# A layernorm, long-convolution and feed-forward kernel: Strassen's seven products in the first feed-forward product, 512-column second product, chunks of two tiles

## The chip, the cores and the metric

The kernel runs on one core of a Trainium2 chip. The metric is the device time of one execution in microseconds (us); the kernel before was timed in three runs, which gave a median of 1087.03 us (1082.56 to 1088.22). All values are float32. TensorE (PE) multiplies, VectorE (DVE), ScalarE (ACT) and GpSimd (POOL) work on elements, and SyncE (SP) issues most transfers. Matmuls write to PSUM, whose eight banks of 512 float32 columns are the scarce resource in what follows.

## The reference

```python
x  = A_q                                    # [1, 2048, 576]
xn = _layernorm(x)                          # over the last axis
# A: q * (long causal convolution of (short convolution of k) * v, plus kv * ssm_D)
k_shift = sum(k_pad[:, t:t + S, :] * shift_k[:, ks - 1 - t] for t in range(4))
kv = k_shift * v
y  = irfft(rfft(kv, 2S) * rfft(ssm_k, 2S))[:, :S] + kv * ssm_D
# B: feed-forward, 576 -> 4608 -> 576
h  = jnp.maximum(jnp.einsum("bsd,df->bsf", xn, w1), 0)
out = x + xn * y + jnp.einsum("bsf,fd->bsd", h, w2)
```

## The kernel before

**Products in three passes.** A float32 factor is held as two fp32r parts, a high one (`hi`, `h1`, `hh`) and the rest (`lo`, `l1`, `ll`). A product of two such factors is three matmuls: high by high, high by low, low by high. ACT makes the high part by a copy, and DVE or POOL subtracts it from the source to make the low part. ACT and DVE read results out of PSUM.

**Feed-forward.** The 2048 rows of x are 16 tiles of 128 rows, in four blocks of four tiles (`b`); two blocks make a half. The 4608 hidden columns go in 12 chunks (`ci`) of three tiles of 128 (`FT = 3`), and each half of the rows passes over all of them, so that there are 24 chunk passes. For each chunk, block and tile `mm1` (L322) makes a transposed hidden tile [128 hidden, 512 rows]: the 576 input columns are four contraction tiles of 128 and a remainder of 64, which takes 4 x 3 + 2 = 14 matmuls of 512 columns (L334, output `psh`). ACT applies the ReLU into `hh` (L339) and DVE makes `ll` (L340). `mm2` (L344) multiplies a row tile's hidden part by the chunk's three tiles of w2: two column halves of 288, each 3 x 3 = 9 matmuls (L358, output `pso`), and DVE adds each half into `acc` in SBUF (L362 for a half's first block, L366 otherwise). The `mm2` of a block run while the next block's `mm1` do.

**Operands.** `make_xT` (L244) takes statistics of four row tiles (L168), normalizes (L183), transposes on PE (L269) into `psf` and splits the columns (L203, L204); `first_xT` (L212) does this for the first block, with a centring that does not wait for the standard deviation, whose reciprocal is applied later at L362. `split_w1` and `split_w2` (L306, L315, and POOL at L277) make the weights' two parts, one chunk ahead; `load_w1` and `load_w2` refill the single raw buffer on SP's queue.

**The convolution.** `conv` (L411) is a generator that does the long convolution as an FFT by matmuls in four stages: `fk` transforms the kernel, `fx` makes the short convolution and the gate (DVE at L483 to L492) and transforms it, `fm` multiplies in the middle (32 groups, L562, with ACT copies at L583 to L617), `fo` transforms back (L700, L701), multiplies by the normalized x and adds. Stages hand over through DRAM (`zx`, `zk`, `zy`). For the row tiles of the second half, which `fo` does first, the result is added into `acc` (L673), where the feed-forward also adds.

**What sets the order.** `tick` advances `conv` by a share of the matmul columns issued, so that its pieces lie between the feed-forward's in program order. The tile scheduler then orders each engine by a simulated timeline, within the data dependencies; on the chip each engine runs its own list in order. PSUM has two banks for `psh`, three for `pso` and three for `psf`.

## Time and profile before

| | us |
|---|---|
| median of 3 runs | 1087.03 (1082.56 to 1088.22) |
| span of the profiled execution | 1084.4 |
| TensorE busy | 1070.8 (99% of the span) |
| VectorE busy | 732.5 (68%) |
| ScalarE busy | 585.0 (54%) |
| GpSimd busy | 261.9 (24%) |

A row of a group view reads: line, engine, operation, output <- inputs, sizes, count, then busy time in us and the mean in ns of one. Matmuls overlap each other in PE's pipeline, so that a matmul's own duration is longer than the spacing of two; spacings are read from stretches of the chain or the timeline. DVE's operations overlap by a little too: the groups add up to some 770 us where 732.5 are busy. The window view gives, for each stretch, its length, the busy time of PE, weight loads, DVE, ACT and POOL with instruction counts, the granted TensorE clock as a share of full speed, the share of DMA time and GB/s.

### The profile page before, as it was taken

Reading aid. Unit: us, or ns where it says so; the run is one execution under the profiler, and the core shown is the slowest. Engines: PE = TensorE matmul, PEld = TensorE weight load, DVE = VectorE, ACT = ScalarE, POOL = GpSimd, SP = SyncE. Lnnn points to the kernel's source line nnn. Section 1 sums busy time; section 2 is a strip of 40 time slices with the busy share of each in tenths; the row PEclk is TensorE's granted clock in tenths of the full one; section 3 lists DMA queues with packets and bytes.
Section 4 is the critical chain, followed back from the end, with each engine's and each line's share of the span. In section 5 each row is a group of like instructions: output and inputs, shape, how many; then the busy total and the mean of one; then the engine's idle time right before and its main releaser. Section 6 shows DMA issues by size and latency. Waiting matters only on the chain.

```text
span 1084.4 us, 17301 instructions
## 1 busy us (share of the span) xinstructions
PE 1070.8 (99%) x6537; PEld 977.2 (90%) x6537; DVE 732.5 (68%) x1213; ACT 585.0 (54%) x1184; POOL 261.9 (24%) x218
## 2 busy tenths in 40 slices
PE   8999999999999999999999999999999999999998
PEld 5889899998999999999999999899999999999998
DVE  5423677949998777677666676666656666876774
ACT  4221587823443323333388787888788864543430
POOL 4131222412312322312213031211113032332410
PEclk9999999999999999999999999999999999999999
DMA  9950345664644525325564343434344227745524
GB/s 217 181 145 27 119 147 190 195 185 133 187 138 136 153 77 164 117 60 171 190 182 135 99 135 99 135 99 136 92 143 141 80 103 221 201 130 143 164 81 110
DMA packets 112255, 150.79 MB, mean 139 GB/s; under 512 B 45261, under 2 KB 62927, under 8 KB 112172
## 3 DMA queue, kind: packets, MB, share of 16 engines
q1 hardware_dynamic: 103884, 135.50, 42.0%
q0 software_dynamic: 7968, 13.44, 4.8%
q8 instruction: 52, 0.85, 0.3%
q10 hardware_dynamic: 320, 0.74, 0.3%
q14 instruction: 31, 0.25, 0.1%
HBM read 114.26 MB, written 35.39 MB: 138 GB/s over the span
## 4 chain that ended last, share of the span: by engine, by line
PE 90%; DMA 4%; SPq 2%; DVE 2%; ACT 1%; issue 1%; POOL 0%; ACTq 0%; DVEq 0%
PE pso L358 40%; PE psh L334 39%; PE psf L562 7%; PE psf L398 3%; DMA r<-in_w 3%; SPq L421 2%; PE psf L700 1%; PE psf L701 1%; DMA k-1_2414<-in_k 1%; DMA sk<-in_shift_k 0%; PE psf L269 0%; DVE lok L553 0%; POOL l L277 0%; DVE k L611 0%; DVE lox L553 0%
## 5 line engine op out<-in xcount | busy, mean ns | idle before, releaser
L277 POOL TENSOR_TENSOR l<-r,h 128x640 fp32r<-128x640 f32 (+1 forms) x144 | 224.4, 1563 | 621.8 <-ACT h L306 448.3
L358 PE MATMUL pso<-h,hh 128*128 128x288 f32 x1152 | 337.3, 295 | 3.7 <-ACT hh L339 2.7
L358 PE MATMUL pso<-l,hh 128*128 128x288 f32 x1152 | 338.5, 295 | 0.0
L358 PE MATMUL pso<-h,ll 128*128 128x288 f32 x1152 | 337.7, 295 | 0.0
L334 PE MATMUL psh<-xhi,h 128*128 128x512 f32 x576 | 226.5, 394 | 1.1 <-DVE ll L340 1.1
L334 PE MATMUL psh<-xlo,h 128*128 128x512 f32 x576 | 226.5, 393 | 0.0
L334 PE MATMUL psh<-xhi,l 128*128 128x512 f32 x576 | 225.8, 392 | 0.0
L358 PEld LDWEIGHTS pso<-h,hh 128*128 128x128 f32 x1152 | 215.8, 188 | 10.4 <-ACT hh L339 3.4
L358 PEld LDWEIGHTS pso<-l,hh 128*128 128x128 f32 x1152 | 216.3, 188 | 5.8
L358 PEld LDWEIGHTS pso<-h,ll 128*128 128x128 f32 x1152 | 216.0, 188 | 0.6
L366 DVE TENSOR_TENSOR acc<-pso,acc 128x288 f32<-128x288 f32 x288 | 128.6, 451 | 75.1 <-PE pso L358 72.1
L339 ACT ACTIVATE hh<-psh 128x512 fp32r<-128x512 f32 x144 | 85.6, 595 | 169.1 <-PE psh L334 168.2
L340 DVE SCALAR_TENSOR_TENSOR ll<-psh,hh 128x512 fp32r<-128x512 f32 x144 | 99.0, 687 | 109.8 <-ACT hh L339 109.5
L334 PEld LDWEIGHTS psh<-xhi,l 128*128 128x128 f32 x576 | 108.4, 188 | 20.3
L334 PEld LDWEIGHTS psh<-xhi,h 128*128 128x128 f32 x576 | 108.4, 188 | 17.1 <-DVE ll L340 1.4
L334 PEld LDWEIGHTS psh<-xlo,h 128*128 128x128 f32 x576 | 108.6, 188 | 15.5 <-DVE xlo L204 0.4
L315 ACT ACTIVATE h<-r 128x576 fp32r<-128x576 f32 x72 | 48.9, 682 | 73.4 <-DMA r<-in_w 46.9
L362 DVE SCALAR_TENSOR_TENSOR acc<-pso,rstd,acc 128x288 f32<-128x288 f32 x96 | 48.3, 512 | 27.5 <-PE pso L358 26.5
L392 DVE TENSOR_TENSOR ks<-kt,ks 64x288 fp32r<-64x288 f32 x64 | 57.6, 901 | 3.3 <-ACT ks L391 1.3
L399 ACT ACTIVATE zx<-psf 128x288 f32<-128x288 f32 x64 | 25.8, 407 | 59.3 <-PE psf L398 38.9
L334 PE MATMUL psh<-xhl,l 128*128 128x512 f32 x144 | 56.4, 392 | 0.0
L334 PE MATMUL psh<-xhl,h 128*128 128x512 f32 x144 | 56.2, 391 | 0.0
(109 smaller groups left out, 1451.2 us busy)
## 6 DMA issues: line engine op xcount, KB each, us to landing
r<-in_w SPq DMA_DIRECT2D x24, 864.0 KB, 5.3
r<-in_w SPq DMA_DIRECT2D x23, 768.0 KB, 6.1
zk<-zk SPq DMA_DIRECT2D x32, 288.0 KB, 2.5
zx<-zx SPq DMA_DIRECT2D x32, 288.0 KB, 2.6
ztk<-zk SPq DMA_DIRECT2D x32, 288.0 KB, 3.0
ztx<-zx SPq DMA_DIRECT2D x32, 288.0 KB, 2.8
zy<-vo SPq DMA_DIRECT2D x32, 288.0 KB, 2.1
zo<-zy SPq DMA_DIRECT2D x32, 288.0 KB, 3.0
```

Source lines behind the costliest of these rows:

```text
L277: return nc.gpsimd.tensor_tensor(dst, src, hi, OP.subtract)
L315: nc.scalar.activation(h2, r2[:, j, :], AF.Copy)
L334: nc.tensor.matmul(ps, a, m, start=i == 0, stop=i == len(seq) - 1)
L339: done["act"] = nc.scalar.activation(hh, ps, AF.Relu)
L340: lows.append(nc.vector.scalar_tensor_tensor(ll, ps, 0.0, hh, op0=OP.max, op1=OP.subtract))
L358: nc.tensor.matmul(ps[:, :NH], a[:, cols], m[:, dc], start=n == 0, stop=n == 3 * FT - 1)
L362: done["acc"] = nc.vector.scalar_tensor_tensor(acc[t][:, dc], ps[:, :NH], rstd[:, t:t + 1], acc[t][:, dc], op0=OP.mult, op1=OP.add)
L366: done["acc"] = nc.vector.tensor_tensor(acc[t][:, dc], ps[:, :NH], acc[t][:, dc], OP.add)
L392: nc.vector.tensor_tensor(dst[other], src[own], dst[own], OP.subtract)
L398: nc.tensor.matmul(ps[:, :NH], w[:, u, n, :], stk, start=n == 0, stop=n == 1)
L399: nc.scalar.activation(z, ps[:, :NH], AF.Copy)
L562: nc.tensor.matmul(ps[:, :NH], a, m[:, cols], start=n == 0, stop=n == 2)
```

## The change

Chunks have two tiles (`FT = 2`): 18 chunks, 36 chunk passes. In the first chunk of each half, `mm1` stays as it was (14 matmuls a tile, of 512 columns). In the other 34 passes `quad` treats the two hidden tiles, the half's two row blocks and two of the four full contraction tiles as a 2 x 2 by 2 x 2 product, done with seven products instead of eight (Strassen's scheme in Winograd's form). The other two contraction tiles and the remainder (`rest`) are plain: 8 matmuls for each of the four outputs. That is 7 x 3 + 4 x 8 = 53 matmuls a pass instead of 56.

Sums of operands: `combine_w` makes S1 to S4 on DVE in the raw weight buffer each pass; `combine_x` makes T1 to T4 on DVE, with splits on ACT and DVE, once a half. Sums of results are made in PSUM: `al` is a bank of its own (`ps_a`, named `psa`), filled by an ACT copy of `ka` and then accumulated on by matmuls; DVE writes `th = al + e5` and `ka = al + e5`. To give that bank, `pso` has two instead of three.

`mm2` does 512 of the 576 columns in one group (6 matmuls of 512 columns, one DVE addition of 512). The last 64 columns are computed transposed by `mm2_rest`: 4 matmuls of 512 columns a block, added up in `accT`, and at the end of each half transposed back (4 PE transposes, 8 small DVE additions a block). `first_xT` now normalizes fully. `DRAINS` spreads ten pieces of the previous pass's second product over the six parts of `quad`. Some buffers of `conv` shrink (`stk` 5 to 3, `k` 6 to 5, `hi` and `lo` 4 to 3, `ft` 3 to 2).

```diff
-FT = 3
+FT = 2
+STEP = 3
+DM = 512
+DRAINS = (1, 2, 2, 2, 2, 1)
...
-    ps_o = ctx.enter_context(tc.tile_pool(name="ps_o", bufs=3, space=PSUM))
+    ps_a = ctx.enter_context(tc.tile_pool(name="ps_a", bufs=1, space=PSUM))
+    ps_o = ctx.enter_context(tc.tile_pool(name="ps_o", bufs=2, space=PSUM))
...
+    def combine_x(bi):
+        v1, v2 = pieces(f"va{bi}")
+        v3, v4 = pieces(f"vb{bi}")
+        for v, p, q in ((v1, b12, b11), (v3, b22, b12)):
+            tt(v, p[0], q[0], OP.subtract)
+            tt(v, v, p[1], OP.add)
+            tt(v, v, q[1], OP.subtract)
+        split(t1, v1)
+        for v, p, q in ((v2, b22, v1), (v4, b21, v2)):
+            tt(v, p[0], q, OP.subtract)
+            tt(v, v, p[1], OP.add)
+        for t, v in ((t2, v2), (t3, v3), (t4, v4)):
+            split(t, v)
...
     def first_xT(srcs):
+        for t0 in range(0, BT, 2):
+            for t in (t0, t0 + 1):
+                stats(t, srcs[t])
+            inv_std(t0, 2)
+            for t in (t0, t0 + 1):
+                normalized(xn[t], srcs[t], t)
...
+    def combine_w(ci):
+        s1, s2, s3, s4, a12, a22, a11, a21 = (r1[:, n, :] for n in range(8))
+        with tc.issue_after(lows[-1].ins):
+            nc.vector.tensor_tensor(s1, a21, a22, OP.add)
+            nc.vector.tensor_tensor(s3, a11, a21, OP.subtract)
+            nc.vector.tensor_tensor(s2, s1, a11, OP.subtract)
+            nc.vector.tensor_tensor(s4, a12, s2, OP.subtract)
...
+    def quad(ci):
+        th = bank(f"pst{ci}")
+        run_seq(th, product(w["s1"], x["t1"]), True, True)
+        nc.scalar.activation(e5, th, AF.Copy)
+        ka = bank(f"psk{ci}")
+        run_seq(ka, product(w["a11"], x["b11"]), True, True)
+        nc.scalar.activation(al, ka, AF.Copy)
+        yield
+        run_seq(al, product(w["s2"], x["t2"]), False, True)
+        nc.vector.tensor_tensor(th, al, e5, OP.add)
+        run_seq(ka, product(w["a12"], x["b21"]) + rest(ci, 0, 0), False, True)
+        relu(ci, 0, 0, ka)
+        yield
+        run_seq(al, product(w["s3"], x["t3"]), False, True)
+        nc.vector.tensor_tensor(ka, al, e5, OP.add)
+        yield
+        run_seq(al, product(w["a22"], x["t4"]) + rest(ci, 1, 0), False, True)
+        relu(ci, 0, 1, al)
+        yield
+        run_seq(th, product(w["s4"], x["b22"]) + rest(ci, 0, 1), False, True)
+        relu(ci, 1, 0, th)
+        yield
+        run_seq(ka, rest(ci, 1, 1), False, True)
+        relu(ci, 1, 1, ka)
...
+    def mm2_rest(ci, b):
+        ps = ps_o.tile([P, 512], F32, tag="o", name=f"psr{ci}_{b}")
+        seq = [(weights[ci]["w2", j][:, DM:2 * D - DM], m) for j in range(FT)
+               for m in hid[ci, b % HB, j]]
+        run_seq(ps, seq, True, True)
...
+        ps = ps_o.tile([P, 512], F32, tag="o", name=f"pso{ci}_{t}")
+            seq += [(hh[:, cols], wh), (hh[:, cols], wl), (ll[:, cols], wh)]
+        run_seq(ps, seq, True, True)
...
+                parts = quad(ci)
+                for n, take in enumerate(DRAINS):
+                    next(parts)
+                    drain(take)
+                    next(ahead)
```

Three places of the new order on DVE matter for what follows. In the names, `pso_8` is the second product of row tile 8, `psr` its last columns, `ll_1_0` the low part of block 1, tile 0; the last number only counts tiles.

The first place is the `fx` stage, where DVE does the short convolution (`e`, `c`, `xs`). Before, a piece of a chunk reads:

```order
L340 SCALAR_TENSOR_TENSOR ll_1_2_4085<-psh_1_2_4058,hh_1_2_4084 128x512
L362 SCALAR_TENSOR_TENSOR acc_94<-pso_2_0_4088,rstd,acc_94 128x288
L362 SCALAR_TENSOR_TENSOR acc_94<-pso_2_1_4099,rstd,acc_94 128x288
L362 SCALAR_TENSOR_TENSOR acc_94<-pso_3_0_4110,rstd,acc_94 128x288
L362 SCALAR_TENSOR_TENSOR acc_94<-pso_3_1_4121,rstd,acc_94 128x288
L486 TENSOR_TENSOR e_2_4136<-k_3607,sk 128x576
L487 TENSOR_TENSOR c_4066<-c_4066,e_2_4136 128x576
L486 TENSOR_TENSOR e_3_4153<-k_3426,sk 128x576
```

Now it reads:

```order
L419 SCALAR_TENSOR_TENSOR ll_1_1_3395<-psk_3174,hh_1_1_3394 128x512
L342 TENSOR_TENSOR r_13_3331<-r_13_3331 128x128
L343 TENSOR_TENSOR r_13_3331<-r_13_3331 128x128
L479 TENSOR_TENSOR accT_523<-psr_1_3311,accT_523 128x512
L623 TENSOR_TENSOR c_3324<-k_3259,sk 128x576
L507 TENSOR_TENSOR acc_231<-pso_4_3317,acc_231 128x512
L626 TENSOR_TENSOR e_1_3350<-k_3090,sk 128x576
L344 TENSOR_TENSOR r_13_3331<-r_13_3331 128x128
L507 TENSOR_TENSOR acc_231<-pso_5_3359,acc_231 128x512
```

The sums of the weights (`r_13`), the last columns (`accT`) and wider additions have come between the convolution's pieces, and the weight sums, whose input is a load, stand ahead of PSUM reads.

The second place is the change of halves, where the second half's first block is prepared. Before:

```order
L366 TENSOR_TENSOR acc_220<-pso_7_1_5179,acc_220 128x288
L168 BN_STATS bn_5197<-xn_4990 128x6 x2
L168 BN_STATS bn_5201<-xn_4990 128x6 x2
L168 BN_STATS bn_5205<-xn_4993 128x6 x2
L168 BN_STATS bn_5209<-xn_4993 128x6 x2
L169 BN_AGGR mv<-bn_5197 128x2
L169 BN_AGGR mv<-bn_5201 128x2
L169 BN_AGGR mv<-bn_5205 128x2
L340 SCALAR_TENSOR_TENSOR ll_1_0_5287<-psh_1_0_5265,hh_1_0_5286 128x512
```

Now:

```order
L507 TENSOR_TENSOR acc_231<-pso_4_4789,acc_231 128x512
L174 BN_STATS bn_4812<-xn_4664 128x6 x2
L174 BN_STATS bn_4816<-xn_4664 128x6 x2
L174 BN_STATS bn_4820<-xn_4667 128x6 x2
L174 BN_STATS bn_4824<-xn_4667 128x6 x2
L507 TENSOR_TENSOR acc_231<-pso_5_4899,acc_231 128x512
L175 BN_AGGR mv<-bn_4812 128x2
L175 BN_AGGR mv<-bn_4816 128x2
L507 TENSOR_TENSOR acc_234<-pso_6_4907,acc_234 128x512
```

The statistics stood after a finished block of second products, with a first product's `ll` next; now they stand in the middle of four second products in a row.

The third place is the start of `fo`, where the convolution's result is added into `acc` (L673 before, L813 now). Before:

```order
L366 TENSOR_TENSOR acc_5707<-pso_13_1_10316,acc_5707 128x288
L657 TENSOR_TENSOR olo_10311<-zo_10231,ohi_10310 128x576
L665 SCALAR_TENSOR_TENSOR y_10133<-xt_10012,mv,y_10133 128x576
L703 TENSOR_TENSOR y_10220<-psf,low_0_10221 64x288
L673 SCALAR_TENSOR_TENSOR acc_5701<-y_10133,rstd,acc_5701 128x576
L340 SCALAR_TENSOR_TENSOR ll_2_2_10376<-psh_2_2_10342,hh_2_2_10375 128x512
L703 TENSOR_TENSOR y_10220<-psf,low_1_10263 64x288
L366 TENSOR_TENSOR acc_5710<-pso_14_0_10379,acc_5710 128x288
```

Now:

```order
L843 TENSOR_TENSOR y_9173<-psf,low_1_9220 64x288 x2
L805 SCALAR_TENSOR_TENSOR y_9173<-xt_9081,mv,y_9173 128x576
L797 TENSOR_TENSOR olo_9280<-zo_9184,ohi_9279 128x576
L843 TENSOR_TENSOR y_9272<-psf,low_0_9273 64x288 x2
L813 SCALAR_TENSOR_TENSOR acc_5312<-y_9173,rstd,acc_5312 128x576
L797 TENSOR_TENSOR olo_9340<-zo_9230,ohi_9339 128x576
L797 TENSOR_TENSOR olo_9394<-zo_9283,ohi_9393 128x576
L843 TENSOR_TENSOR y_9272<-psf,low_1_9333 64x288
L507 TENSOR_TENSOR acc_5312<-pso_8_9491,acc_5312 128x512
```

Before, second products of tiles 13 and 14 were being read when the result for tiles 8 and 9 (`acc_5701`) came. Now the second product of tile 8 itself is read only after the convolution's result for tile 8 has been added into the same `acc_5312`.

More of the change, by code (lines that the diff above doesn't have):

```diff
@@ new lines, in f32, with split, pieces @@
+    def f32(t):
+        return t[:].bitcast(F32)
+    def combine_x(bi):
+        b11, b21, b12, b22 = ([f32(m) for m in ops[n]] for n in ("b11", "b21", "b12", "b22"))
+        t1, t2, t3, t4 = (operand(f"t{n}") for n in range(1, 5))
+        tt = nc.vector.tensor_tensor
+        def split(t, v):
+            nc.scalar.activation(t[0], v, AF.Copy)
+            tt(t[1], v, t[0], OP.subtract)
+        def pieces(name):
+            pair = xp.tile([P, 2, D], F32, tag="xn", name=name, bufs=BT // 2)
+            return pair[:, 0, :512], pair[:, 1, :512]
+        v1, v2 = pieces(f"va{bi}")
[10 more added lines that the diff above has]
+            split(t, v)
@@ L211, in first_xT @@
     def first_xT(srcs):
-        xT_tiles(0)
+        plain_tiles(0)
         ps = []
@@ L817, in h3_ffn_kernel @@
+            for _ in range(6):
+                next(ahead)
+            if ci:
+                drain(10)
+                behind = second(ci, half)
+    drain(10)
     rest_of_stream()
```

378 lines of the change are left out of this document (226 added, 152 removed).

## The prediction

> **What bounds the kernel now.** I read the page's head and its chain first.
>
> ```profile
> span 1084.4 us, 17301 instructions
> PE 1070.8 (99%) x6537; PEld 977.2 (90%) x6537; DVE 732.5 (68%) x1213; ACT 585.0 (54%) x1184; POOL 261.9 (24%) x218
> PE 90%; DMA 4%; SPq 2%; DVE 2%; ACT 1%; issue 1%; POOL 0%; ACTq 0%; DVEq 0%
> ```
>
> TensorE is nearly the whole chain. A busy PE need not be a fed one, so the waits of PE come next (engine and line, what it waited for, total us, times, longest).
>
> ```profile
> PE pso L358 <- ACT hh L339: 2.7, 2, 2.5
> PE psf L234 <- DVE xn L189: 2.2, 1, 2.2
> PE pso L358 <- DVE acc L366: 0.9, 1, 0.9
> ```
>
> In 1084 us PE waits a few us for other engines. The windows (start:end, length, busy PE, PEld, DVE, ACT, POOL, clock, DMA, GB/s) say how near the others are to binding.
>
> ```profile
> 0.00:15.00 15.00, 11.59 (x46) 6.17 (x46) 4.11 (x12) 6.57 (x12) 4.21 (x10) 0.90 0.90 224
> 30.00:60.00 30.00, 27.49 (x151) 23.76 (x150) 11.84 (x23) 8.07 (x14) 7.41 (x5) 0.94 0.99 192
> 230.00:480.00 250.00, 249.06 (x1503) 227.14 (x1502) 197.56 (x291) 86.99 (x160) 64.47 (x50) 1.00 0.46 139
> 300.00:400.00 100.00, 100.00 (x611) 91.72 (x610) 82.12 (x121) 36.10 (x67) 23.35 (x19) 1.00 0.43 132
> 480.00:540.00 60.00, 60.00 (x379) 55.19 (x377) 39.84 (x87) 20.85 (x41) 15.67 (x11) 1.00 0.52 158
> 580.00:880.00 300.00, 298.68 (x1877) 276.53 (x1876) 195.94 (x326) 243.47 (x538) 58.47 (x37) 1.00 0.37 116
> ```
>
> DVE's 68% is an average. In the `fx` stage (230 to 480) it is 79% busy, in its densest 100 us 82%; in `fm` (580 to 880) ACT is 81%. PE is full in all of them, also at the change of halves (480 to 540). So the kernel is bound by PE's work, with DVE close behind in one stage and ACT in another.
>
> **PE's work: -18 us.** The chain gives the spacing of matmuls (start, us, group).
>
> ```profile
> 67.47 3.57 PE pso L358 x27
> 97.01 3.19 PE psh L334 x14
> 102.58 3.18 PE psh L334 x14
> 161.92 3.20 PE psh L334 x14
> ```
>
> A matmul of 288 columns takes 3.57 / 27 = 0.132 us of the stream, one of 512 columns 3.20 / 14 = 0.229. Before: 12 chunks x 4 blocks x 3 tiles x 14 = 2016 of 512 and 12 x 16 x 18 = 3456 of 288, that is 461 + 457 = 918 us. After: 4 x 14 x 2 + 34 x 53 = 1914 in the first product, 18 x (16 x 6 + 4 x 4) = 2016 in the second, all of 512: 3930 x 0.2286 = 898 us. The first product saves 23 us and the second costs 4 more, because the last 64 columns take four matmuls of 512 for each block and chunk. With 16 added transposes (some 0.1 us each) the balance is -18 us. The convolution's 960 matmuls of 288 (127 us) stay.
>
> The Trainium skill, page "TensorE: Matmul & The Clock Gate", section "Back-to-back issue gap", gives N / 2.4 + 2.5 ns a matmul: 215.8 and 122.5 ns, by which the saving would be about 10 us and not 18. The rows above have a fixed part of some 8 ns, so the trace decides for 18.
>
> **DVE's work: +10 us in `fx`.** Prices come from the groups of the trace (mean ns of one after the busy us).
>
> ```profile
> L366 DVE TENSOR_TENSOR acc<-pso,acc 128x288 f32<-128x288 f32 x288 | 128.6, 451 | 75.1 <-PE pso L358 72.1
> L362 DVE SCALAR_TENSOR_TENSOR acc<-pso,rstd,acc 128x288 f32<-128x288 f32 x96 | 48.3, 512 | 27.5 <-PE pso L358 26.5
> L340 DVE SCALAR_TENSOR_TENSOR ll<-psh,hh 128x512 fp32r<-128x512 f32 x144 | 99.0, 687 | 109.8 <-ACT hh L339 109.5
> L178 DVE TENSOR_TENSOR q<-q 128x4 f32<-128x4 f32 x4 | 1.4, 342 | 0.1
> L486 DVE TENSOR_TENSOR e<-k,sk 128x576 f32<-128x576 f32 x42 | 40.2, 957 | 0.3
> L487 DVE TENSOR_TENSOR c<-c,e 128x576 f32<-128x576 f32 x48 | 39.6, 825 | 1.3
> L339 ACT ACTIVATE hh<-psh 128x512 fp32r<-128x512 f32 x144 | 85.6, 595 | 169.1 <-PE psh L334 168.2
> ```
>
> Before, the feed-forward took 128.6 + 48.3 + 99.0 = 276 us of DVE, 7.7 us for each 1/36 of the work. Now each of 36 passes has 8 additions of 512 columns, 2 of the transposed rest, 4 `ll` and 2 result sums: 16 x 0.687 = 11.0 us, at the price of the other 512-column read of PSUM. The four weight sums of 128 columns lie between L178's 0.342 (4 columns) and 0.687; they are nearer the former, 1.4 us in all. That is 12.4 us a pass, +4.7, and over the kernel +169 us. A pass takes (898 + 127) / 36 = 28.5 us of PE, so `fx` holds 8.8 passes: 197.6 + 41 = 239 us of DVE in 250, and 82.1 + 16.5 = 98.6 in its densest 100. Counting the new order row by row with the durations of the groups, less 0.05 us of overlap each, three passes early in `fx` (9 to 11) come to 86 us of DVE, 37 for the feed-forward and 49 for pieces of the convolution like L486 and L487, beside 78 us of PE. That is +8 by itself. Behind it stand the weight sums: a chunk's raw buffer is single, and the load that refills it takes about this long.
>
> ```profile
> r<-in_w SPq DMA_DIRECT2D x23, 768.0 KB, 6.1
> ```
>
> It starts when POOL has split the pass's last rest of w1, and DVE reaches the sums some 4 us later, right after the last `ll`; the wait of about 2 us holds the PSUM reads behind it on DVE, and PE needs those with only two `pso` banks. Where DVE has slack this is covered; in `fx` there is none. I take +10 for the stage, from 0 (DVE's order just fits) to 25 (2 us in every pass besides).
>
> **The start: +8.** Before, the first block is centred without the standard deviation (time, us, engine).
>
> ```profile
> 10.39 0.82 DVE L168 BATCH_NORM_STATS2 bn<-acc 128x6 f32<-128x288 f32 x2 [2.53 <-DMA acc<-in_x]
> 14.29 0.79 PE L334 MATMUL psh<-xhi,h 128*128 128x512 f32 x1
> 19.73 0.75 DVE L175 TENSOR_SCALAR q<-mv 128x4 f32<-128x4 f32 x1
> 23.27 0.18 DVE L180 RECIPROCAL rstd<-q 128x4 f32<-128x4 f32 x1
> ```
>
> The second pair of tiles lands at 10.4. DVE then does their statistics (about 1.9 us), the chain to `rstd` (19.73 to 23.45, 3.7 us), the other pair's share of both (1.5) and four normalizations (0.58 each, 2.3; row below): transposes end near 19.5 and the first product starts near 20.5, 6 us later. Then DVE has 28 us of rows (second block, then T1 to T3) before the first `al` accumulation, which PE reaches after about 25 us of work: some 5 us more. The stretch from 30 to 60 was idle for 2.5 us anyway, on loads that stay. Net +8, from 4 to 14.
>
> **The change of halves: +9.** Each of the two blocks puts on DVE 8 statistics, the chain, four normalizations and five splits, and the second one T1 to T4 (10 sums and 4 splits of 512 columns, near 9 us).
>
> ```profile
> L168 DVE BATCH_NORM_STATS2 bn<-xn 128x6 f32<-128x288 f32 x16 | 6.1, 444 | 3.1 <-DMA xn<-in_x 3.0
> L183 DVE TENSOR_SCALAR xn<-acc,mv,rstd 128x576 f32<-128x576 f32 x4 | 2.1, 576 | 0.0
> L183 DVE TENSOR_SCALAR xn<-xn,mv,rstd 128x576 f32<-128x576 f32 x8 | 6.3, 850 | 0.0
> ```
>
> The same statistics (3.1 us in a row) and normalizations (3.4 us) cost PE nothing before. Now they fall among four second products in a row, and two banks let PE go 2.7 us ahead, so each of four such clumps stalls it by 1 to 3 us; the transposed rest, PE to DVE to PE in each block, adds about 1.5 twice. From 0, as before, to 17.
>
> **The seam from `fm` to `fo`: +17.** The new order makes `acc<-pso_8` wait for the convolution's result of tile 8, and PE has `pso_9`, then 15 us of other rows (among them the last 27 products of `fm` in one run), before `pso_10`, which needs that bank. The chain to the result in the trace of before (timeline):
>
> ```profile
> 893.26 0.76 DVE L590 TENSOR_TENSOR yl<-k,yh 128x576 fp32r<-128x576 f32 x1
> 903.54 1.43 DVE L657 TENSOR_TENSOR olo<-zo,ohi 128x576 fp32r<-128x576 f32 x2 [2.34 <-ACT ohi L656]
> 916.65 0.80 DVE L673 SCALAR_TENSOR_TENSOR acc<-y,rstd,acc 128x576 f32<-128x576 f32 x1
> ```
>
> And two groups of ACT's copies in `fm`:
>
> ```profile
> L583 ACT ACTIVATE k<-psf 64x288 f32<-64x288 f32 x64 | 25.5, 398 | 5.8 <-PE psf L562 5.1
> L552 ACT ACTIVATE hix<-ztx 128x576 fp32r<-128x576 f32 x32 | 21.9, 685 | 0.7
> ```
>
> From the last group's `yl` to the first `olo` it is 10.3 us (a store and a load through DRAM), from there to the addition 9 (DVE's rows in the new order) to 14. When PE stands at the weight of this pass, ACT's order still has 36 copies like L583, 7 like L552 and a few others, 23 us, ahead of that. So the bank comes free 20 us (if ACT has run ahead) to 43 us into a pass in which PE has 21 us to do. I take +17, nearer the far end because the run of 27 products shows that `fm` lags here; from 0 to 28, with DVE's 37 us of rows in this pass.
>
> **Other handovers: +4.** `al` is an ACT copy (0.6 us by L339) that PE needs one or two product groups later (0.9 to 1.4 us); the reuse of `ka` from pass to pass goes through ACT and DVE (1.3 us) behind one group and three matmuls (2.1 us). Both are covered when the queues are empty; 0.1 us in each of 34 passes is 4, from 0 to 10. ACT gains 34 x 2 x 0.6 = 41 us of copies and some 18 us of splits, which brings `fm` to 87%: covered. POOL (24%), the smaller `conv` buffers, the weights' bytes (unchanged) and the end (the last addition in two pieces, as before) I take at nothing.
>
> **Sum.** 1084.4 - 18 + 10 + 8 + 9 + 17 + 4 = 1114.4; the profiled execution lies 2.6 us below the median of the runs, so the time is 1117 us.
>
> **The rivals.** *The list schedule absorbs it.* The scheduler fills PE's list with whatever its timeline has ready, and before it did so without a wait in all the same places. Then only the start (+4) and a little of `fx` (+3) remain: 1087 - 18 + 7 = 1076, faster by 1%. Against it stands DVE at 98.6% where PE was 100%. Chance 0.20. *The gains and waits cancel* (seam at 0, halves at 0): 1082 to 1092, 0.06. *DVE becomes the bound everywhere.* Its busy time would be 732.5 + 169 + 20 (T sums and halves) = 921 us; in-order queues and two banks may keep it from more than 80%, about what its densest stretch had with PE full: 921 / 0.8 = 1151. For it speaks that every pass now couples PE and DVE in both directions, against it that `fm` has DVE at only 65% + 16%. It decides if DVE idles in `fk` and `fm` while PE waits too. Chance 0.17, 1140 to 1165.
>
> The Trainium skill, the same page, section "The HAM clock gate", has the array at half rate after an idle window of about 3.4 us, until as long a busy one. The row from 30 to 60 (0.94) shows some of it. By it the seam and two or three other long waits would cost about 1.7 us more each, some 5 us, which the sum leaves out.
>
> **How the numbers follow.** The forecast, 1095 to 1135 around 1117, has 0.57. The range for 8 in 10 reaches into both rivals, 1076 to 1155. A measurement of this kernel tells 0.5% from no change. Faster by more than that (below 1081.6): 0.20; within: 0.06; slower: 0.74.
>
> **What would show it.** PE busy should fall below 95%, with 3930 matmuls of 512 columns spaced 0.229 us where they run. PE's waits should name DVE `acc` (L507) and gaps should lie at the start, in `fx`, at the halves and, as one wait over 10 us, before `pso_10` at the beginning of `fo`. DVE should be near 900 us. The first product should start near 20 us. I am wrong if PE stays above 98% busy; wrong in the sizes if the seam shows no long gap, or if waits are spread evenly over all passes.

## The result, and the profile after

The changed kernel takes 1161.33 us (median of 4 runs, 1159.42 to 1163.36) where the kernel before took 1085.34 (median of 4 runs): 1.070 times as long, 95% interval 1.067 to 1.073. It is slower, as forecast, but by 76 us and not by 30. The span of the profiled execution is 1160.0 us. One execution of a later variant, the mixed order, took 2723 us and is left out of that variant's figure. First the page's head and its chain of work.

```profile
span 1160.0 us, 15021 instructions
PE 1088.1 (94%) x5011; PEld 892.3 (77%) x5011; DVE 887.2 (76%) x1461; ACT 639.4 (55%) x1293; POOL 338.6 (29%) x328
PE 76%; DVE 7%; DMA 6%; SPq 3%; issue 3%; ACT 2%; POOL 2%; DVEq 0%; POOLq 0%; ACTq 0%
```

PE has 1526 matmuls fewer, yet falls from 99% to 94% of a longer span, and from 90% to 76% of the chain. Its waits (engine and line, what it waited for, total us, times, longest):

```profile
PE pso L397 <- DVE acc L507: 10.6, 11, 3.7
PE psf L840 <- DMA xt<-in_x: 8.5, 1, 8.5
PE psb L483 <- DVE accT L479: 6.7, 4, 3.9
PE psh L397 <- DVE xl L218: 6.0, 1, 6.0
PE psf L271 <- DVE xn L189: 5.5, 1, 5.5
```

They are few and long. To place all lost time, take windows by stage (length, busy PE, PEld, DVE, ACT, POOL with counts, clock, DMA, GB/s).

```profile
0.00:60.00 60.00, 42.29 (x161) 29.36 (x162) 36.38 (x83) 17.15 (x33) 18.73 (x26) 0.86 1.21 180
60.00:240.00 180.00, 178.74 (x829) 148.07 (x828) 128.08 (x201) 113.42 (x203) 58.04 (x60) 1.00 0.41 125
240.00:480.00 240.00, 230.46 (x1032) 188.45 (x1031) 213.85 (x319) 94.37 (x177) 83.29 (x72) 0.99 0.50 145
480.00:600.00 120.00, 107.71 (x484) 86.19 (x483) 94.94 (x180) 50.32 (x101) 32.49 (x29) 0.94 0.43 123
600.00:930.00 330.00, 329.35 (x1636) 279.08 (x1635) 245.19 (x401) 267.89 (x584) 83.15 (x72) 1.00 0.38 114
930.00:1020.00 90.00, 68.45 (x282) 54.48 (x281) 60.24 (x95) 48.76 (x103) 21.13 (x23) 0.79 0.50 144
1110.00:1160.00 50.00, 41.07 (x181) 32.10 (x179) 30.95 (x57) 5.05 (x10) 6.79 (x10) 0.99 0.28 71
```

"Lost" below is a stretch's length less what its matmuls need at the spacing of a full PE: 0.2286 us for 512 columns, 0.1322 for 288, 0.1 for a transpose. In 930 to 1020, 101 of the 282 matmuls are the convolution's: 181 x 0.2286 + 101 x 0.1322 = 54.7, so 35.3 of 90 us are lost (35.5 if the matmul that was running at 930 is not counted, as below). Done so for both kernels:

| stage | lost before | lost after | more | forecast |
|---|---|---|---|---|
| start, to 60 us | 14.3 | 28.3 | 14.0 | 8 |
| `fx` | 1.9 | 15.1 | 13.2 | 10 |
| change of halves | 0.6 | 20.4 | 19.8 | 9 |
| seam from `fm` to `fo` | 0 | 35.5 | 35.5 | 17 |
| end (last 50 us; before: last 4) | 4.3 | 10.6 | 6.3 | 0 |
| all other passes | 5.0 | 9.5 | 4.5 | 4 |
| PE's work at full spacing | 1058.4 | 1040.6 | -17.7 | -18 |

The sum is +75.6, as the spans differ. Of the 34 stretches from one pass of seven products to the next, 23 lose 1 us or less. All places but the end are those of the prediction; six terms of its sum, the end's nothing among them, cost more than it said, two of them far more. At the change of halves (480 to 600) PE's two largest waits are:

```profile
PE psb L483 <- DVE accT L479: 5.1, 2, 3.9
PE pso L397 <- DVE rstd L186: 3.4, 1, 3.4
```

The first is the transposed rest on its way back (called the flush below), which waits for its last sum (`psb` is the bank of its transposes). The second is a wait behind the statistics of one of the second half's blocks.

The largest loss is the seam. Pieces of the chain of work there (start, us, piece), and the windows of 10 us:

```profile
952.76 0.77 DVE k L755
956.94 2.06 DMA zy<-vo
962.96 6.98 DMA zo<-zy
970.74 0.77 DVE olo L797
971.53 6.20 DMA zo<-zy
979.28 0.73 DVE acc L813
980.01 0.61 DVE acc L507
980.67 2.93 PE pso L397 x6
986.49 1.36 PE pso L397 x6
```

```profile
950.00:960.00 10.00, 3.86 (x12) 2.58 (x12) 3.10 (x5) 3.84 (x9) 0.18 (x1) 0.52 0.16 59
960.00:970.00 10.00, 3.59 (x12) 2.92 (x12) 4.74 (x8) 3.52 (x7) 1.98 (x4) 0.50 1.05 265
970.00:980.00 10.00, 7.83 (x20) 5.55 (x20) 8.93 (x16) 6.15 (x12) 0.66 (x2) 0.50 1.06 307
```

The addition of `fo`'s result into `acc` (L813) must come before the feed-forward's own (L507), whose bank PE needs for the six `pso` matmuls at 980.67. Behind 946 PE's list holds only `fm`'s last products, which wait for ACT's copies, then `fo`'s first, which wait for the round trip through DRAM. The clock is at half for 30 us: six such matmuls take 2.93 us at 980.67 and 1.36 at 986.49.

This chain is that of the second result bank, for tile 9. The first, for tile 8, came free 5 us earlier. Rows of VectorE on the way (start, us):

```profile
954.33 0.76 DVE L730 TENSOR_TENSOR yl<-k,yh 128x576 fp32r<-128x576 f32 x1 [0.81 <-ACT yh L757]
963.02 1.43 DVE L797 TENSOR_TENSOR olo<-zo,ohi 128x576 fp32r<-128x576 f32 x2 [7.94 <-ACT ohi L796]
972.27 0.80 DVE L813 SCALAR_TENSOR_TENSOR acc<-y,rstd,acc 128x576 f32<-128x576 f32 x1
974.93 0.69 DVE L507 TENSOR_TENSOR acc<-pso,acc 128x512 f32<-128x512 f32 x1
```

They are the last `yl` of `fm`, the first `olo` of `fo`, the addition of tile 8's result and the read of `pso_8` behind it; PE's next `pso` matmuls begin at 975.68.

### The profile page after: what moved, and what is told of

Same layout as the page of the kernel before. It is cut to its first block, busy times and chain, and to the rows that moved or that the text cites. A ratio compares the mean times of both kernels' runs of the same rounds, so it can differ in the third digit from the quotient of the medians.

```text
span 1160.0 us, 15021 instructions
## 1 busy us (share of the span) xinstructions
PE 1088.1 (94%) x5011; PEld 892.3 (77%) x5011; DVE 887.2 (76%) x1461; ACT 639.4 (55%) x1293; POOL 338.6 (29%) x328
## 4 chain that ended last, share of the span: by engine, by line
PE 76%; DVE 7%; DMA 6%; SPq 3%; issue 3%; ACT 2%; POOL 2%; DVEq 0%; POOLq 0%; ACTq 0%
PE pso L397 29%; PE psk L397 13%; PE psa L397 10%; PE pst L397 8%; PE psf L702 6%; PE psr L397 5%; DMA r<-in_w 3%; PE psf L538 2%; SPq L561 2%; DMA zo<-zy 1%; DVE acc L507 1%; POOL w L311 1%; DMA sk<-in_shift_k 1%; DVE ll L419 1%; DMA fin<-acc 1%
## 5 line engine op out<-in xcount | busy, mean ns | idle before, releaser
L397 PE MATMUL pso<-w,hh 128*128 128x512 f32 x1152 | 371.8, 400 | 17.5 <-DVE acc L507 10.6
L397 PEld LDWEIGHTS pso<-w,hh 128*128 128x128 f32 x1152 | 214.4, 191 | 65.7 <-DVE acc L507 15.9
L507 DVE TENSOR_TENSOR acc<-pso,acc 128x512 f32<-128x512 f32 x289 | 196.9, 683 | 62.4 <-PE pso L397 61.1
L397 PE MATMUL pso<-w,ll 128*128 128x512 f32 x576 | 229.1, 398 | 0.0
L311 POOL TENSOR_TENSOR w<-r,w 128x512 fp32r<-128x512 f32 (+1 forms) x144 | 140.5, 1004 | 141.9 <-ACT w L384 141.8
L311 POOL TENSOR_TENSOR gbl<-r,gbh 128x384 fp32r<-128x384 f32 x72 | 83.7, 1162 | 250.1 <-ACT gbh L376 231.7
L397 PEld LDWEIGHTS pso<-w,ll 128*128 128x128 f32 x576 | 110.1, 191 | 22.8
L311 POOL TENSOR_TENSOR gal<-r,gah 128x896 fp32r<-128x896 f32 (+1 forms) x38 | 78.8, 2073 | 158.4 <-ACT gah L355 118.9
L397 PE MATMUL psr<-hh,w 128*128 128x512 f32 x144 | 57.3, 398 | 2.6 <-DVE acc L507 2.5
L397 PE MATMUL psr<-ll,w 128*128 128x512 f32 x144 | 56.9, 395 | 0.2 <-DVE ll L419 0.2
L419 DVE SCALAR_TENSOR_TENSOR ll<-psk,hh 128x512 fp32r<-128x512 f32 x68 | 46.6, 685 | 13.9 <-ACT hh L418 13.4
```

What stands on the lines that cost most here:

```text
L311: return nc.gpsimd.tensor_tensor(dst, src, hi, OP.subtract)
L397: nc.tensor.matmul(ps, a, m, start=start and i == 0, stop=stop and i == len(seq) - 1, skip_group_check=not start)
L419: lows.append(nc.vector.scalar_tensor_tensor(ll, ps, 0.0, hh, op0=OP.max, op1=OP.subtract))
L507: done["acc"] = nc.vector.tensor_tensor(acc[t][:, dc], ps[:, dc], acc[t][:, dc], OP.add)
```

## The experiments

Unless said otherwise an edit is made to the changed kernel, and every kernel was timed in four runs. "Loses" is counted as above, by pass of the feed-forward. Spans and medians differ by up to 4 us.

### The places, one by one

**First half first in `fo`.**

```diff
-            order = [*range(HT, T), *range(HT)]
+            order = [*range(T)]
```

> Only the order in which the convolution finishes its row tiles is changed: first half first, so that the feed-forward's additions to acc of tiles 8 to 15 no longer wait for the first results of fo. Theory (the seam is a wait of the result bank for acc, which waits for fo's first result, some 20 us of latency through DRAM): the loss between 940 and 1000 us, 29.7 us in the changed kernel, falls below 8, DVE and PE work stay, and the span is 1130 to 1138 instead of 1160. Rival (the convolution itself is late there and PE has nothing else, or DVE limits the stretch): the gap before the first product of fo stays, and the span is within 5 us of 1160.

Measured: 1143.8 us, span 1140.3. The two passes at the seam, which lost 29.5 and 6.3, lose 0.2 and 0.1; from 921 to 979 us PE does not wait once:

```profile
921.00:954.00 33.00, 33.00 (x167) 28.16 (x167) 21.87 (x38) 26.26 (x58) 8.28 (x7) 1.00 0.17 58
954.00:979.00 25.00, 25.00 (x118) 20.85 (x117) 15.56 (x28) 11.07 (x22) 8.84 (x10) 1.00 0.69 191
979.00:1012.00 33.00, 30.55 (x136) 24.79 (x135) 28.92 (x48) 17.34 (x34) 14.02 (x17) 0.95 0.76 225
1044.00:1080.00 36.00, 33.23 (x149) 25.91 (x148) 33.59 (x59) 19.21 (x39) 14.12 (x15) 1.00 0.69 187
```

So the order on `acc` makes the seam. But the three passes from 979 to 1080 lose 14.9 where they lost 1.0, with VectorE busy 88 to 93%, and the end 2.6 more: of 35.5 us, 20 are gained.

**The second chunk's w1 on GpSimd's queue.**

```diff
-            queue = nc.gpsimd if ci == 0 and o == 0 else nc.sync
+            queue = nc.gpsimd if ci == 1 or (ci == 0 and o == 0) else nc.sync
```

> The three loads of the second chunk's first weights are issued on GpSimd's queue instead of SyncE's, where they stood behind 11 issues of the convolution's kernel (26.5 us). Theory (the start's second half is lost because the weight sums wait 8.3 us on VectorE for that load, with the second block's splits behind them): the load lands before 35 us, the loss in 30 to 60 us falls from 14.7 us to below 6 and the span to 1149 to 1154. Rival (VectorE's own 28 us of sums and splits for the second block set that stretch): the wait goes, but PE waits for T1 to T3 as long; the span stays above 1156.

Measured: 1157.4 us. The first pass loses 33.6 us in place of 27.1: the scheduler put the first seven-product matmuls behind the second products of the first chunk, and PE waited 13.4 us for `accT`. The edit changed more than the load; it tells nothing of its cause.

**Weight sums on GpSimd.**

```diff
-        with tc.issue_after(lows[-1].ins):
-            nc.vector.tensor_tensor(s1, a21, a22, OP.add)
...
+        nc.gpsimd.tensor_tensor(s1, a21, a22, OP.add)
...
```

> The four weight sums of every chunk move from VectorE to GpSimd, with no order after the last ll. Theory (in fx the loss of 13.8 us between 250 and 350 us comes from VectorE standing in the sums' wait for their load): that loss falls below 5, the start's wait on VectorE goes as well, and the span is 1140 to 1148, with VectorE's busy time about 40 us lower. Rival (VectorE has too much work in fx, whatever it waits for): the loss in fx falls only by the sums' own 1.1 us a pass, some 4 us, and the span stays above 1150. A second rival: GpSimd, which then waits for the load itself, delays its splits and the convolution's loads, and the span does not fall at all.

Measured: 1153.5 us, VectorE's busy time down by 25 us. The three passes at the beginning of `fx` lose 12.9 us in place of 13.7. The window of the changed kernel, then of this one:

```profile
270.00:300.00 30.00, 28.43 (x131) 23.19 (x129) 29.75 (x43) 13.33 (x27) 11.76 (x10) 1.00 0.50 140
```

```profile
270.00:300.00 30.00, 28.72 (x130) 23.49 (x131) 29.75 (x41) 13.05 (x25) 15.11 (x16) 1.00 0.48 147
```

VectorE is full either way: the theory fell, the first rival holds. The 8 us gained lie at the start, the halves and in single waits.

**The end in free banks.**

```diff
-        ps = ps_o.tile([P, 512], F32, tag="o", name=f"psr{ci}_{b}")
+        final = ci == HALVES * NCHUNK - 1
+        ps = bank(f"psr{ci}_{b}") if final else ps_o.tile([P, 512], F32, tag="o", name=f"psr{ci}_{b}")
...
+            back = (bank(f"psb{b}") if final else
+                    ps_o.tile([P, 512], F32, tag="o", name=f"psb{b}"))
```

> In the last chunk the transposed rest and its transposes use the first product's banks, which are free by then, instead of the two result banks. Theory (the last 16 us lose 8.5 us because PE stands in front of the result banks while the rest goes through accT, the transposes and eight additions, twice): the loss from the end of the convolution on falls by 5 to 7 us, and the span is 1153 to 1155. Rival (the additions on VectorE themselves limit the end): under 2 us.

Measured: 1155.2 us; the last pass loses 6.3 in place of 10.6. The theory holds, with 4 us in place of its 5 to 7.

**The flush in other banks, at both halves.**

```diff
-            back = ps_o.tile([P, BT, 2, D - DM], F32, tag="o", name=f"psb{b}")
+            back = fft_psum().rearrange("p (i n c) -> p i n c", i=BT, n=2)
```

with the last chunk's rest in `bank`, as in the experiment ahead.

> The changed kernel, with the transposed rest's way back through a convolution bank instead of a result bank at both halves, and the last chunk's rest in a bank of the first product. Theory (at the halves PE stands before the result bank that the transposes hold until eight additions are done behind the statistics): the 17.4 us lost in the pass from 495 us fall to 8 to 12, the end gains 4 to 6, and the span is 1146 to 1152. Rival (the statistics and normalizations on VectorE delay the ordinary result additions as much): the halves stay above 15, and only the end's 4 us are gained, 1156.

Measured: 1144.4 us, a little below the theory's range. The pass at the halves loses 11.2 in place of 17.4, the last one 6.0, as the theory had them. The other gains are elsewhere and were not forecast: 5.1 us in the pass behind the seam.

**The kernel's loads held back, first attempt.** The `kt` loads were put under `tc.issue_after(done["pool"].ins)`.

> The 16 loads of the convolution's kernel (kt) may start only after GpSimd has split the first chunk's second weights, so that the second chunk's w1, whose buffer is free at 22.4 us, is no longer issued behind them at 38.3. Theory (the second half of the start's loss is VectorE standing 8.3 us in the weight sums' wait for that load): the load lands before 32 us, the first pass's loss of 27.1 us falls to 17 to 20, and the span is 1150 to 1153. Rival (VectorE's 28 us of sums and splits for the second block set the first products): the loss stays above 24 and the span above 1156.

Measured: 1161.1 us. The loads' order on SyncE's queue stayed as it was, as its rows show (start, us, queue, line, count):

```profile
11.67 27.80 SPq L562 DMA_DIRECT2D kt<-in_ssm_k  x11
39.66 1.92 SPq L324 DMA_DIRECT2D r<-in_w  x1
```

So the run did not test what it was meant to.

**The kernel's loads held back by data.**

```diff
             kt = fp.tile([P, NH, A2], F32, tag="kt", name="kt", bufs=1)
+            with tc.issue_after(done["pool"].ins):
+                nc.gpsimd.memset(kt[:, ::KD, 0], 0.0)
```

> A small memset of kt on GpSimd, behind the split of the first chunk's second weights, holds back all 16 kt loads, so that on SyncE the second chunk's loads are issued ahead of them. Theory (half of the start's loss is the weight sums' wait for that load on VectorE): the load lands before 32 us, the first pass's loss of 27 us falls to 19 to 22, and the span is 1152 to 1156. Rival (VectorE's rows for the second block and T1 to T3 set the first seven products): the wait of 8.3 us goes, the loss stays above 25 and the span above 1157.

Measured: 1152.2 us. In the changed kernel, VectorE stood in the first weight sum until 45.28 (first row); here it does it at 25.48 without a wait, because the load went out at 21.72 (the other rows):

```profile
45.28 0.29 DVE L342 TENSOR_TENSOR r<-r 128x128 f32<-128x128 f32 x1 [8.26 <-DMA r<-in_w]
```

```profile
21.72 0.40 SPq L324 DMA_DIRECT2D r<-in_w  x1
25.28 34.21 SPq L563 DMA_DIRECT2D kt<-in_ssm_k  x16
59.61 1.90 SPq L324 DMA_DIRECT2D r<-in_w  x1
25.48 0.29 DVE L342 TENSOR_TENSOR r<-r 128x128 f32<-128x128 f32 x1
66.13 0.29 DVE L342 TENSOR_TENSOR r<-r 128x128 f32<-128x128 f32 x1 [6.88 <-DMA r<-in_w]
```

The first pass loses 17.9 in place of 27.1, as the theory had it. But the third chunk's load now stands behind 34 us of `kt` issues, and the second pass loses 9.2 in place of 2.0. The wait has moved by a chunk. Of the 9 us gained in all, the first two passes hold 2 and later passes the rest, so that the time lies in the theory's range by luck.

**The pieces of `fx` spread.**

```diff
-            yield -PAUSE
+            yield -1.5 * PAUSE
             for n in range(KS):
                 tap(0, n)
-                yield -PAUSE / 8
+                yield -PAUSE / 4
```

and likewise to the second tile's taps; the constant `PAUSES`, by which the pauses are allowed for, goes from 16 to 17.6.

> At the beginning of fx the pauses between the convolution's first pieces are doubled (an eighth to a quarter of PAUSE) and the one behind its first loads is 1.5 times as long. Theory (the 14 us lost in the three passes from 243 us are these pieces in a bunch on VectorE, 49 us in three passes, and the 7.8 us in which it stands before the first window): they lose 4 to 8 us and the span is 1150 to 1155. Rival (VectorE is short of time in the whole of fx): the loss spreads over the later passes of fx and the span stays within 3 us of 1160.

Measured: 1161.7 us. The three passes lose 10.6 in place of 13.7, the six behind them 6.0 in place of 1.7: 16.6 in the stage, against 15.4. The rival holds: `fx` lacks VectorE time as a whole.

### Parts of the change alone

**Plain first product.** `quad`, `combine_w` and `combine_x` go; each pass has four `mm1` of 14 matmuls.

```diff
-                parts = quad(ci)
-                for n, take in enumerate(DRAINS):
-                    next(parts)
+                for n, take in enumerate((2, 3, 3, 2)):
+                    mm1(ci, n // 2, n % 2)
                     drain(take)
```

> The second half of the change alone: the first product is plain (four products of 14 matmuls a pass in place of the seven, so 102 matmuls of 512 columns more, 23.3 us of PE, and no T sums, no weight sums, no al); the second product, the transposed rest and the two result banks stay as in the changed kernel. Theory (the waits come from the two result banks and the order on acc, so the seam's some 30 us, the flush at the halves and the end stay, while the start and fx get better by 10 to 15 us): span 1160 + 23 - 10 to 15 = 1165 to 1175. Rival (the seven products couple PE, ACT and VectorE and are the cause of most losses): the losses fall to about the 26 us of the kernel before, and the span is 1085 to 1110.

Measured: 1160.5 us, the time of the seven products, with 23.3 us more PE work. It loses 23.1 us to 52 us, 12 in `fx` from 253 to 349 us, 25.3 at the seam and 7.9 in the last 30 us. The time is 5 us below the theory's range and far above the rival's: the seven products save PE work and lose it again.

**Plain first product, three result banks.** As before, and:

```diff
-    ps_a = ctx.enter_context(tc.tile_pool(name="ps_a", bufs=1, space=PSUM))
-    ps_o = ctx.enter_context(tc.tile_pool(name="ps_o", bufs=2, space=PSUM))
+    ps_o = ctx.enter_context(tc.tile_pool(name="ps_o", bufs=3, space=PSUM))
```

> As the plain first product with the 512-column second product, but the bank that al held is given to the second product: three result banks, as in the kernel before. Theory (the third bank is what covers an additions' clump of some 3 us on VectorE): the losses in fx and at the halves fall to below 10 us together, the seam loses under 15 us, and the span is 1100 to 1120, against 1165 to 1175 with two banks. Rival (the order on acc alone makes the seam, and a bank more is filled at once): the seam stays at 25 us or more and the span is 1135 or more.

Measured: 1132.4 us, 28 less than with two. The seam loses 12.2 (6.9 and 5.3), `fx` 6, the halves 9.8; the start's 22.7 stay. Near the theory, above its time by 12.

**Three result banks, two for the convolution.**

```diff
-    ps_o = ... bufs=2, space=PSUM))
-    ps_f = ... bufs=3, space=PSUM))
+    ps_o = ... bufs=3, space=PSUM))
+    ps_f = ... bufs=2, space=PSUM))
```

> The changed kernel with three result banks, the third taken from the convolution's three. Theory (two result banks are what lets a clump on VectorE reach PE): fx and the halves, 14 and 17 us lost, fall below 8 each; the seam falls by 5 to 10 us, since PE gets one more second product done ahead of the wait; the convolution's two banks cost 5 us or less; span 1125 to 1140. Rival (the convolution needs its third bank): a loss of 0.3 us or more in every pass of fm and fo appears, 10 us or more in all, and the span is 1155 or more.

One more of the first block's transposes goes to a result bank with it.

Measured: 1226.5 us. Both expectations missed it: `fm` runs as well as ever (0.2 to 0.9 us lost a pass), but `fx` loses 25 us and the pass of the seam 84.4. Its window, then PE's longest waits of one kind in the whole run, of which 21.0 us fall into this window:

```profile
932.00:1071.00 139.00, 90.12 (x340) 70.67 (x338) 75.25 (x122) 100.25 (x224) 11.02 (x12) 0.67 0.41 122
```

```profile
PE psf L702 <- ACT k L726: 21.9, 19, 1.8
```

With nothing of the feed-forward to fill in, PE goes through `fm`'s rest one ACT copy at a time and through `fo`'s beginning behind VectorE's additions and one load, at a mean clock of 0.67.

**The kernel before with two result banks.**

```diff
-    ps_o = ctx.enter_context(tc.tile_pool(name="ps_o", bufs=3, space=PSUM))
+    ps_o = ctx.enter_context(tc.tile_pool(name="ps_o", bufs=2, space=PSUM))
```

> The kernel before with two result banks in place of three and nothing else changed. Theory (the third bank covers VectorE's clumps, and the plain product gained 28 us by it): the span rises by 15 to 35 us, to 1100 to 1120, with PE's waits on acc in fx, at the halves and in fo. Rival (two banks cost only in the order that the change makes): within 5 us of 1084.

Measured: 1098.5 us, ratio 1.014 (1.012 to 1.016): 15 us, the low end of the theory. It has no seam: the loss is 1 to 4 us a stretch of 30 in `fx` and at the halves. The bank costs 15 us where no long wait meets it, 28 where one does.

**The kernel before with chunks of two tiles.** `FT = 2`, and the table of splits:

```diff
+SPLITS = {(0, 1): ((1, 0),), (1, 0): ((1, 1), (2, 0)), (1, 1): ((2, 1),)}
+SPLITS0 = {(1, 0): ((1, 0), (1, 1)), (1, 1): ((2, 0), (2, 1))}
```

> The kernel before with chunks of two tiles (FT = 2) in place of three, and the table of the splits adapted; PE's work is the same, VectorE's result additions rise from 384 to 576, some 90 us. Theory (a smaller first chunk gives PE less to do before the second block's operands are there, and VectorE has less room in fx): 4 to 8 us at the start and 3 to 8 in fx, span 1091 to 1100. Rival (with three banks and the second product in halves both stay covered): within 3 us of 1084.

Measured: 1169.9 us, far above both. The first 60 us lose 24.1 in place of 14.3, about what the plain kernels lose there. The rest is spread over the kernel, with PE waiting 19 us, in 18 waits, for `ll`. This order now drains three second products in a row behind a block's last tile, where it was two, so the run says that the old order does not suit such chunks, not what they cost in the changed one.

### The repairs together

**Three repairs:** first half first, weight sums on GpSimd, the flush in other banks.

> The changed kernel with three repairs together: first half first in fo, weight sums on GpSimd, the flush in other banks. Theory (separate places, each with its own cause, so the gains add; and the 13.6 us that the first-half-first order lost again between 980 and 1080 us, with VectorE at 93%, hold some 5 us of waits of the sums for their load, which go too): 1160 - 20 - 8 to 14 - 16 = 1110 to 1116. Rival (one cause behind all, VectorE's work, so that each repair only moves the loss on): 1125 or more.

Measured: 1127.1 us. By the medians the single gains add up to 42 us; 34 came, and the time is in the rival's range. The places are as the single repairs left them: the seam loses 0.7, `fx` 12.7 in its three passes, the pass at the halves 10.9. What does not add lies behind the seam: `fo`'s later passes still lose 14.0, so the sums' waits were not what held them, and the end 9.5 in place of 6.0.

**Four repairs:** also the first attempt at the `kt` loads.

> As the three repairs, with the kt loads behind the second weights' split of the first chunk as well. Theory: 7 to 10 us below the three repairs, all of it in the first 60 us. Rival: within 3 us of them, since with the sums on GpSimd VectorE no longer waits for that load.

Measured: 1127.7 us, no difference; that edit did nothing.

**A mixed order:** as the four, with `order = [*range(4), *range(HT, T), *range(4, HT)]`.

> As the four repairs, with fo's order 0 to 3, 8 to 15, 4 to 7 in place of 0 to 15. Theory (four tiles of lead, some 25 us, cover fo's latency through DRAM, and the additions to acc of 8 to 15 no longer fall together with the last chunk): no seam, and 3 to 8 us less than the four repairs, from the last 100 us. Rival (the lead is too short, or VectorE's total work in fo, whatever its order, sets these stretches): within 3 us, or above the four repairs.

Measured: 1140.6 us, the median of three runs, above the four repairs. A loss of the seam's size comes back, 30.0 us in the pass from 971, but from another cause: of PE's waits there only 0.8 us are for `acc`, and 16.7 are for VectorE's `y` (L844). Windows there, and the chain:

```profile
1000.00:1010.00 10.00, 5.73 (x17) 3.99 (x17) 9.34 (x16) 5.64 (x12) 5.75 (x8) 0.50 1.08 288
1010.00:1020.00 10.00, 3.01 (x8) 1.61 (x7) 4.24 (x8) 2.82 (x6) 1.65 (x4) 0.50 0.73 212
```

```profile
998.49 6.09 DMA r<-in_w
1004.72 1.47 POOL r L341
1008.40 0.54 POOL out L158
1008.94 6.65 DMA out<-y
1015.67 0.46 DVE y L844
```

`fo`'s store, issued by GpSimd, stands behind the weight sums there, which wait for their load; VectorE waits for the buffer that the store frees, and PE for VectorE, at half clock for 20 us. The repair on GpSimd has a price of its own.

**All repairs:** the three, the `kt` loads held back by data, `fx`'s pieces spread.

> The changed kernel with all repairs: first half first, weight sums on GpSimd, the flush in other banks, the kt loads behind w1, fx's pieces spread. Theory (the places add): the three repairs' 1127 less 5 to 8 at the start and 6 to 10 in fx, 1110 to 1116; slower than the kernel before. Rival: within 5 us of 1127.

Measured: 1130.9 us. The rival holds. Against the three repairs the start is the same (25.9 us in two passes, 26.4 there), `fx` loses 13.6 in place of 15.2 and the halves 9.7 in place of 16.0, but one pass of `fo` loses 19.4 in place of 2.4.

**The plain product with repairs:** three result banks, first half first, the flush in other banks, the `kt` loads held back by data.

> The plain first product with three result banks, first half first, the flush in other banks, the kt loads behind w1. Its PE work is 23 us above that of the seven products. Theory (the bank is worth more than the products removed): 1132 - 10 (seam) - 8 (halves) - 4 (end) = 1105 to 1112, below or equal to all repairs of the seven products. Rival (without the sums it gains as little from repairs that the seven products gain more from): 1120 or more, above them.

Measured: 1121.8 us, the fastest of the changed kernel's variants, and slower than the kernel before (1.035, 1.033 to 1.037). The time is the rival's, 1120 or more; that it is below the seven products is the theory's. With 23 us more PE work than the seven products it is 5 us faster than the best of their repairs:

```profile
span 1118.1 us, 14872 instructions
PE 1090.7 (98%) x5113; PEld 901.8 (81%) x5113; DVE 773.9 (69%) x1229; ACT 593.9 (53%) x1251; POOL 312.3 (28%) x363
```

From 571 to 1030 us no pass loses more than 0.4 us. No version beats the kernel before, so none is offered.

## Why the prediction was right in direction and wrong in size

The time lies beyond the wide range, 1076 to 1155, too. Term by term:

- **PE's work, -18.** The counts came out as forecast and give -17.7 at the spacing forecast; the row `986.49` above has 1.36 / 6 = 0.227 at full clock. Right. The Trainium skill's figure for an isolated gap ("TensorE: Matmul & The Clock Gate", section "Back-to-back issue gap"), 0.2158, is below this spacing and those of the rows in the prediction.
- **`fx`, +10.** Measured 13.2, inside its bounds. Its first part was right: too much VectorE work, shown by the full window with and without the sums, and by the loss that only spread when the pieces did. Its second, the sums waiting on their load, was not what held this stage.
- **The start, +8.** Measured 14.0, at its far end. The first product came at 18.9 (forecast 20.5). The cause named for its second part, VectorE's rows for T1 to T3, holds 5 us of the 28.3 at most: the plain product, which has neither these nor weight sums, still loses 23 us there, and the old kernel with chunks of two tiles 24. So most of the start seems to come with the small first chunk, which gives PE less to do while the second block is made ready. The load behind 27 us of `kt` issues adds to it.
- **Other handovers, +4.** Measured 4.5. Right in size; no experiment tells whether it is these handovers.
- **The halves, +9, and the seam, +17.** Measured 19.8 and 35.5, beyond the far ends of 17 and 28. The mechanisms were right (the first half first in `fo` took the seam away, the flush in other banks a third of the halves' loss), but **these two terms are the step that failed**: both waits were there and both were priced too low. At the halves the clumps of statistics came out as priced: PE's waits behind them and for `acc` are 3.4 and 2.8 us, of 6 forecast. The flush was priced at 1.5 us twice, but its transposes wait 5.1 us, and moving its bank gained 6; some 4 us more are matmuls at half clock. At the seam the bank was to come free 20 to 43 us into a pass; it did at 975.7, 54 us after the pass began at 921.4. Two links of that chain came out as priced: from the last `yl` to the first `olo` 8.7 us (10.3 forecast), from there to the addition 9.3 (9 to 14). The link ahead of them was short: the last `yl` came 33 us into the pass, where the prediction had ACT's copies at 23 at most. It had added up the copies as if they ran in a row, but ACT was busy for 26.4 of the 33 us, and otherwise waited for PE's and VectorE's pieces of the same groups. Another 3.4 us, for the addition, VectorE's rows behind it and the read of `pso_8`, had no price. PE had work until 946, then stood in `fm`'s rest and before `fo`, and ran at half clock.
- **The end, 0.** Measured 6.3: the flush again, twice, with nothing beside it. It had been costed as the kernel before ended, though the change puts a chain PE-VectorE-PE-VectorE there.
- **The half clock, left out.** The prediction quoted the Trainium skill's section "The HAM clock gate" and put some 5 us beside the sum. Adding up, for each matmul whose row has the half-rate length, its spacing beyond the full one gives some 20 us (18 to 23, by which rows are still counted as half rate), against 2 to 4 before: about 9 at the seam, 4 in the start's second half and 4 at the halves. It is part of the losses above, and the sum had nothing for it.
- **The rivals.** The list schedule did not absorb it. "VectorE bound everywhere" named the range in which the time fell, 1140 to 1165, but not its cause: its sign was PE waiting in `fk` and `fm` too, and PE runs at 99 to 100% in 60 to 240 and 600 to 930. That it came nearer is luck.

What stays open: how many of the start's 14 us are the load, since holding back `kt` only moved the wait; and what the last 10 us at the halves hang on, which stay with three banks too. With three banks alone 6.5 of them are one wait of the flush's transposes for `accT`; in the plain product with repairs, which has the flush in other banks as well, 9.5 us are lost there, of which 3.1 are the longest wait, on `acc`. That chunks of two tiles cost at the start is shown for the order of the kernel before; that it is PE's want of work there is argued.

## What to carry to other kernels

A saving of matmuls that costs a PSUM bank is to be priced with the bank: here 23 us of PE work were bought with a result bank worth 15 to 28. Where two streams add into one accumulator, the order of the additions ties one stream to the other's longest latency; put the late stream's tiles where nothing else adds yet, and leave VectorE room for what then runs together. Price a long wait of TensorE with the half-rate stretch behind it, not by its length alone.

## What the runs showed of the hardware

- The half rate outlasts the wait. From 970 to 980 us PE is busy 7.83 of 10 us and still at 0.50. Its last wait ends at 980.67, and the rows shorten from 0.51 to 0.40 only between 984.30 and 984.65, after 4 us of work without a gap. That agrees with the busy window of about 3.4 us in the Trainium skill ("TensorE: Matmul & The Clock Gate", section "The HAM clock gate"). Yet from 974.96 to 980.05 us PE also worked without a gap, for 5.1 us, and stayed at half rate, so that a stretch of that length does not always bring the full one.

```profile
984.30 0.51 PE L397 MATMUL psr<-ll,w 128*128 128x512 f32 x1
984.65 0.40 PE L397 MATMUL psr<-hh,w 128*128 128x512 f32 x1
```

- A sum of 128 columns took 0.29 to 0.36 us on VectorE and 0.53 to 0.62 on GpSimd (means of the groups), and GpSimd waited 136 us in 34 passes for the load ahead of the first.
- SyncE's 16 issues of `kt` took 34.2 us in a row, 2.1 each, where a weight load's took 0.4 ahead of them and 1.9 right behind them: a queue can be late by its issues alone.
